# An attention and highway kernel on one core: fp32 dummy matmuls, wider key-value products for batch 0, weights cast in blocks of 128 rows, and a new list of steps

## The chip, the cores and the metric

The kernel runs on one core of one Trainium2 chip. The time is what the device takes for one execution, in microseconds (us); smaller is better. The core has five engines with queues of their own: TensorE (PE in the profile, its weight loads PEld), VectorE (DVE), ScalarE (ACT), GpSimd (POOL) and SyncE (SP), which here only issues transfers. 16 DMA engines carry the transfers.

## What is computed

```python
# q, k, v: (8 batches, 8 heads, 576 rows, 64), fp32
q_s = softmax(q, axis=-1)
k_s = softmax(k, axis=2)                     # over the 576 rows
kv  = einsum('bhsd,bhse->bhde', k_s, v)
x   = einsum('bhsd,bhde->bhse', q_s, kv)     # then (8*576, 512): a row is all heads of one token
H   = maximum(x @ w_h, 0)
T   = 1 / (1 + exp(-(x @ w_t + b_t)))
out = T * H + (1 - T) * x                    # (4608, 512), fp32
```

## The kernel before

**Tiles.** The 4,608 tokens are cut into 36 tiles of 128. Each pair of batches makes nine tiles: four of the first batch, four of the second, and one that shares the last 64 rows of both. Products are in fp16 with fp32 sums. Batch 0 and 1 are taken in halves (pairs of heads), so that work can begin before all of a batch has landed.

**Steps.** Everything is a list of named steps, ORDER (line 16). A loop at the end of the kernel walks through it and emits each step's instructions (`does`, from line 512). The scheduler is off: on each engine the instructions stand in the order of the list, and an engine takes them strictly one after another, so the list sets the order of all queues, that of SP included. A step is written `kind_batch_part` or `kind_tile_part`; a letter behind a colon chooses the engine (A is ScalarE, D VectorE, P GpSimd; F means all of it in one instruction).

Per batch *b*:
- `k`, `v`, `q` (lines 181 to 206): SP issues the loads. Batch 0 and 1 come in pieces, named by the first of their head pairs (`v_0_3`) or of their column groups (`q_0_4`). `w_h`, `w_t` (L208) load a weight in two halves of 256 rows, 512 KB each.
- `ek` (L253): ACT takes the exponential of k. `vc` (L259): a cast of v to fp16, beside a column of ones.
- `kv` (L262 to 272): PE multiplies, in products of 64x65 over rows: two row halves times two heads, four quarters of the array. A half of batch 0 or 1 is 36 such products. `kr` and `kn` (L281, L287) divide by the sums.
- `eq` (L307, 302, 298), `qt`, `qc` (L319 and 324, L333): the exponential of q, its turning on PE, the copy out of PSUM.

Per tile *i*:
- `xu` (L361) multiplies by kv; `rs`, `x` (L370, L376) divide, on DVE. `xt` (L384) turns x on PE, `xe` (L391) copies it to SBUF as xT.
- `bw` (L399, L401) puts the bias into the gate's PSUM; `mt` (L411) and `mh` (L419) are the two big products, four matmuls of 512 columns each. `th` takes a tanh on ACT (L433, L435), `dd` (L439) the maximum on DVE, `uu` the gate product, on DVE (L453) or, "lifted", as two instructions on POOL (L450, L451), `oo` (L471) the sum, on POOL, `st` the store, issued by SP.

**Weights.** `whd` (L226) subtracts the identity from a diagonal block of w_h, `whc` (L232) casts it to fp16 with a factor 0.5, `wtc` (L222) casts w_t. A cast takes 256 rows as 128x1024.

**Fills.** `fill_n` (L167) issues n matmuls of a blank tile into an otherwise unused PSUM buffer. They compute nothing that is kept. PE runs 40 of them up to 16.8 us.

**Buffers.** Tiles rotate in pools: three xT, three each of d16, rs, u16 and others in `dp`, six x16, one PSUM buffer shared by `kv` and `xu`.

Of the kernel before, what the change touches and what calls it, by code (L numbers as in the profile page):

```python
# [533 lines left out]
```

## Time and profile before

| | |
|---|---|
| median of 3 runs | 118.77 us (118.72 to 118.85) |
| the profiled execution's own time | 118.69 us |
| its span, first to last instruction | 116.9 us |
| granted PE clock, mean | 0.995 |
| busy: PE, DVE, ACT, POOL | 109.5, 93.3, 90.0, 89.1 us |
| DMA | 40.58 MB, mean 347 GB/s |
| start of kv_1_1, kv_2, kv_3, kv_4, kv_5, kv_6, kv_7 on PE | 23.24, 38.84, 48.7, 59.0, 66.2, 76.2, 92.8 us |
| start of PE's last matmul; end of the last `oo` | 111.8; 113.47 us |

The span is what the trace covers; 1.8 us of the profiled execution's time lie around it. Rows of 40 digits cut the span into slices of 2.9 us, each digit the busy share in tenths. A PE matmul's duration includes its way through the array and overlaps with the next one's, so its cost in a stream is the distance to the next start: 0.216 us for 512 columns, against a duration of 0.379. A landing is the moment at which a load's semaphore has its full count.

### The profile page before, as it was taken

To read this page: it belongs to the slowest core of one execution; us is meant where nothing else is said; L and a number is where in the kernel's file an instruction comes from. 1 tells how busy PE (TensorE), PEld (TensorE's weight loads), DVE (VectorE), ACT (ScalarE), POOL (GpSimd) and SP (SyncE) were. 2 spreads that over 40 slices of the span, in tenths; PEclk is the share of its full clock that TensorE was granted. 3 is DMA by queue.
4 is the path that set the end of the run, shared out by engine and by line. 5 is a ranking of instruction groups with operands and counts; after the bars stand their busy time and mean duration, and the time that the engine had idled before them with its cause. 6 is when DMAs were issued, how large, how long until landed. Compare 5 with 4: busy or idle time off the path is not lost.

```text
span 116.9 us, 3424 instructions
## 1 busy us (share of the span) xinstructions
PE 109.5 (94%) x1351; PEld 61.6 (53%) x1351; DVE 93.3 (80%) x222; ACT 90.0 (77%) x132; POOL 89.1 (76%) x99
## 2 busy tenths in 40 slices
PE   5999987999999999999999999999999999999930
PEld 2354544545665656565665547566564555554520
DVE  5642587589799979979889798988989887899870
ACT  4356461897999999989999999998597998545520
POOL 5022237208996999999999999999989699999960
PEclk9999999999999999999999999999999999999998
DMA  2999999999999999999999999999999956992875
GB/s 42 399 392 377 408 398 385 375 377 379 393 391 397 383 391 393 358 375 387 357 376 360 387 392 363 390 381 383 399 398 217 302 204 270 397 404 115 315 295 179
DMA packets 24195, 40.58 MB, mean 347 GB/s; under 512 B 5362, under 2 KB 11762, under 8 KB 24180
## 3 DMA queue, kind: packets, MB, share of 16 engines
q1 hardware_dynamic: 24032, 40.24, 96.9%
q8 instruction: 10, 0.16, 0.6%
q10 hardware_dynamic: 148, 0.14, 0.4%
q14 instruction: 5, 0.04, 0.1%
HBM read 30.41 MB, written 9.44 MB: 341 GB/s over the span
## 4 chain that ended last, share of the span: by engine, by line
PE 67%; POOL 15%; issue 6%; DVE 5%; DMA 3%; SPq 1%; POOLq 0%; DVEq 0%
PE tps L411 18%; PE gps L419 16%; PE turned L167 9%; POOL o L471 7%; PE xu L361 6%; PE turned L384 5%; PE kv L269 5%; PE qps L324 4%; POOL u L451 4%; DMA out_dram<-o 3%; POOL g L450 2%; PE qps L319 2%; POOL v L259 2%; DVE x L376 2%; PE tps L401 1%
## 5 line engine op out<-in xcount | busy, mean ns | idle before, releaser
L471 POOL TENSOR_TENSOR o<-u,x 128x512 f32<-128x512 f16 (+1 forms) x36 | 40.6, 1143 | 1.6 <-DVE u L453 0.7
L411 PE MATMUL tps<-w16t,xT 128*128 128x512 f16 (+1 forms) x148 | 37.3, 373 | 0.0
L419 PE MATMUL gps<-w16h,xT 128*128 128x512 f16 x144 | 36.8, 379 | 0.5 <-DVE xT L391 0.5
L376 DVE TENSOR_TENSOR x<-xu,rs 128x512 f16<-128x512 f32 (+1 forms) x39 | 25.2, 649 | 2.4
L259 POOL CAST v<-v 128x1152 f16<-128x1152 f32 (+1 forms) x14 | 14.0, 1010 | 14.7 <-DMA v<-in_v_dram 13.7
L439 DVE SCALAR_TENSOR_TENSOR d<-x,gps 128x512 f16<-128x512 f16 x36 | 24.5, 680 | 0.3
L451 POOL TENSOR_TENSOR u<-g,d 128x512 f16<-128x512 f16 x17 | 19.7, 1158 | 1.7 <-DVE rs L370 0.4
L253 ACT ACTIVATE ek<-k 128x576 f16<-128x576 f32 (+2 forms) x15 | 17.9, 1225 | 3.0 <-DMA k<-in_k_dram 3.0
L419 PEld LDWEIGHTS <-xT 128*128 128x128 f16 x144 | 13.0, 98 | 12.3 <-DVE xT L391 1.8
L399 ACT COPY tps<-ball 128x512 f32<-128x512 f32 x28 | 16.6, 597 | 3.5 <-DVE u L453 3.2
L411 PEld LDWEIGHTS <-xT 128*128 128x128 f16 x148 | 13.2, 98 | 10.6 <-DVE xT L391 0.4
L361 PE MATMUL xu<-kvb,eq 128*128 128x130 f16 (+1 forms) x160 | 14.8, 224 | 0.2 <-DVE kvb L287 0.2
L384 PE MATMUL turned<-idh,x 128*128 128x128 f16 x144 | 14.2, 220 | 0.5 <-DVE x L376 0.5
L391 DVE COPY xT<-turned 128x512 f16<-128x512 f16 (+1 forms) x28 | 10.9, 391 | 4.2 <-PE turned L384 3.0
L435 ACT ACTIVATE tps<-tps 128x512 f32<-128x512 f32 (+1 forms) x20 | 11.2, 559 | 3.6 <-PE tps L411 3.3
L453 DVE SCALAR_TENSOR_TENSOR u<-tps,d 128x512 f16<-128x512 f32 (+1 forms) x19 | 12.7, 671 | 1.4 <-ACT tps L435 0.6
L361 PEld LDWEIGHTS <-eq 128*128 128x128 f16 (+1 forms) x160 | 10.0, 100 | 7.3 <-DVE x L376 2.5
L167 PE MATMUL turned<-blank 128*128 128x512 f16 x40 | 12.4, 458 | 1.5 <-POOL blank L149 1.3
L384 PEld LDWEIGHTS <-x 128*128 128x128 f16 x144 | 9.8, 98 | 6.0 <-DVE x L376 2.1
L307 ACT ACTIVATE qe<-q 128x1024 f16<-128x1024 f32 (+3 forms) x9 | 9.4, 1052 | 4.1 <-DMA q<-in_q_dram 4.1
L450 POOL TENSOR_SCALAR g<-th 128x512 f16<-128x512 f16 x17 | 10.6, 621 | 0.9 <-ACT th L433 0.9
L433 ACT ACTIVATE th<-tps 128x512 f16<-128x512 f32 x17 | 10.0, 594 | 0.9 <-PE tps L411 0.9
(48 smaller groups left out, 106.8 us busy)
## 6 DMA issues: line engine op xcount, KB each, us to landing
k<-in_k_dram SPq DMA_DIRECT2D x6, 1152.0 KB, 12.2
v<-in_v_dram SPq DMA_DIRECT2D x6, 1152.0 KB, 12.0
out_dram<-o SPq DMA_DIRECT2D x23, 256.0 KB, 4.0
q<-in_q_dram SPq DMA_DIRECT2D x10, 512.0 KB, 11.5
out_dram<-o SPq DMA_DIRECT2D x6, 512.0 KB, 3.8
k<-in_k_dram SPq DMA_DIRECT2D x4, 576.0 KB, 9.3
q<-in_q_dram SPq DMA_DIRECT2D x2, 1152.0 KB, 14.2
q<-in_q_dram SPq DMA_DIRECT2D x2, 640.0 KB, 10.5
```

The costliest lines, as they stand in the source:

```text
L167: nc.tensor.matmul(spare, blank[:, 0:P], blank, start=True, stop=True, skip_group_check=True)
L253: nc.scalar.activation(t[:, :, c:c + n].rearrange("p j c d -> p c j d"), T[f"k32{b}"][:, c:c + n].rearrange("p c (j d) -> p c j d", j=NJ), ...
L259: copy(v16[b % NV][:, c:c + n, :, 0:D], T[f"v32{b}"][:, c:c + n].rearrange("p c (j d) -> p c j d", j=NJ))
L361: nc.tensor.matmul(dst, turned_q(b, jp, n), kvb[b % NKV][:, hh, kk], start=True, stop=True, skip_group_check=True)
L376: nc.vector.tensor_mul(t[:, k0:k1], sums(i, k)[:, :, :, 0:64], T[f"rs{i}_{k}"][:, 0:k1 - k0].unsqueeze(3).to_broadcast([P, k1 - k0, 4, D]))
L384: nc.tensor.matmul(t[:, n], T[f"x{i}"][:, n0 + n % 2:n0 + 2 * P:2], idh, is_transpose=True, start=True, stop=True, skip_group_check=True)
L399: nc.scalar.copy(t[:, cs], ball[:, cs])
L411: nc.tensor.matmul(T[gate(i, k)][:, cs], T[f"xT{i}"][:, n], w16["t"][:, n, cs], start=False, stop=(n == parts[-1] and not first), skip_gro ...
L419: nc.tensor.matmul(t, T[f"xT{i}"][:, n], w16["h"][:, n], start=(first and n == parts[0]), stop=(n == parts[-1] and not (first and len(part ...
L439: nc.vector.scalar_tensor_tensor(t, T[f"x{i}"], -0.5, T[f"gps{i}"], op0=ALU.mult, op1=ALU.max)
L451: nc.gpsimd.tensor_mul(t, g, T[f"d{i}"])
L471: eng.tensor_add(t[:, cs], T[f"u{i}_{h}"][:, cs], T[f"x{i}"][:, cs])
```

## The change

- **Fills.** `blank` is fp32 now. `fill_n` issues one matmul for every four units, of 128 columns a unit. An fp32 matmul has no weight load of its own in the list. The list has 36 units in 11 instructions, before 40 in 80 (matmul and weight load).
- **Batch 0's products.** One product takes two heads at once: 64 rows, 128 output rows, 130 columns. Half of what it computes (each head's keys with the other head's values) is not read. A half batch is 18 products and 18 weight loads, before 36 and 36. `kr` and `kn` follow the new layout.
- **Weights.** A cast step takes one block of 128 rows: 128x512 instead of 128x1024. Its engines are chosen anew: w_t three times POOL and once ACT, w_h three times ACT and once DVE; two of four `whd` on DVE, before all four on POOL.
- **Buffers.** Five xT instead of three, five d16 instead of three.
- **The list** is new throughout. w_t is loaded ahead of w_h; batch 0's second half is loaded and multiplied first; PE's first weight products are mt_1 and mt_3, before mh_1 and mh_3; q_1_0 is loaded ahead of v_1_2. Up to v_3 the list loads the same set; then v_4 follows k_4 and v_7 follows k_7. 19 tiles are lifted to POOL (before 17); vc_6_0 and vc_7_0 are on ACT (before POOL). PE's program has 2,561 rows (before 2,704).

```diff
@@ -14,50 +14,50 @@
 ORDER = """
-b_0 q_0_0 v_0_1 setupdve k_0_0 b_32 eq_0_0 bsplit setuppool fill_5 fill_8 bp v_0_0 bc qt_0_0 ek_0_1 v_0_3 ek_0_0 k_0_2
-v_0_2 vc_0_3:A bw_1 vc_0_0 ek_0_2 vc_0_2 q_0_4 vc_0_1:D ek_0_3 bw_0 w_h_0 fill_8 qc_0_0 whd_1:P kv_0_0 eq_0_1 w_h_2
-w_t_2 kr_0_0 whd_0:P whd_2:P w_t_0 k_1_2 v_1_2 q_1_0 k_1_0 v_1_0 fill_5 q_1_4 kn_0_0 q_2_0 k_2_0 eq_0_2 xu_0_0 v_2_0
-q_3_0 rs_0_0 whc_0:A x_0_0 k_3_0 fill_4 v_3_0 kv_0_1 fill_3 kr_0_1 kn_0_1 xu_0_1 rs_0_1 xu_1_0 rs_1_0 qt_0_1 x_1_0
-fill_6 whd_3:P qc_0_1 xt_1_0 xu_3_0 qt_0_2 qc_0_2:A xe_1_0:D fill_1 rs_3_0 x_3_0 x_0_1 xt_3_0 xu_2_0 rs_2_0 x_2_0
-wtc_2:P whc_2:A mh_1_0 wtc_0:P vc_1_3 ek_1_3 ek_1_2 vc_1_0 xe_3_0:D mh_3_0 dd_1 xt_0_1 xt_0_0 mt_1_0 xe_0_0:D mh_0_0
-xe_0_1 dd_3 xt_2_0 mh_0_1 mt_0_1 th_1_0 xe_2_0:D dd_0 vc_1_2:A kv_1_1 uu_1_0 oo_1_0 eq_1_0 mt_0_0 th_0_0 ek_1_0 ek_1_1
-kr_1_1 bw_3 qt_1_0 vc_1_1:A kn_1_1 qc_1_0 mt_3_0 xu_5_1 uu_0_0 mh_2_0 th_3_0 bw_2 rs_5_1 x_5_1 dd_2 xu_4_1 kv_1_0
-kr_1_0 eq_1_1 rs_4_1 xt_5_1 mt_2_0 th_2_0 kn_1_0 bw_5 xe_5_1:D x_4_1 xu_5_0 mt_5_1 qt_1_1 eq_1_2 rs_5_0 x_5_0 xt_5_0
-xu_4_0 bw_4:A uu_3_0:P oo_3_0 xe_5_0:D mh_5_1 rs_4_0 x_4_0 mh_5_0 xt_4_1 qc_1_1:A xt_4_0 xe_4_1:D dd_5 eq_2_0 xe_4_0:D
-v_4_0 mt_5_0 th_5_0 xu_6_0 qt_1_2 rs_6_0 qc_1_2 oo_0_0 mt_4_1 mh_4_1 mh_4_0 uu_2_0:P x_6_0 mt_4_0 eq_2_1 xt_6_0 xu_8_0
-uu_5_0 bw_6:A xe_6_0:D qt_2_0 rs_8_0 x_8_0 mh_6_0 oo_5_0 th_4_0 xt_8_0 dd_4 uu_4_0 xu_7_0 mt_6_0 ek_2_0:F rs_7_0
-vc_2_2:A bw_8 xe_8_0:D mt_8_0 x_7_0 th_6_0 xt_7_0 th_8_0 oo_2_0 vc_2_0 kv_2_0 oo_4_0 qc_2_0 q_4_0 bw_7:A qt_2_1
-qc_2_1:A dd_6 uu_6_0:P oo_6_0 eq_3_0:F xe_7_0:D kr_2_0 kn_2_0 mh_8_0 xu_9_0 rs_9_0 x_9_0 mt_7_0 th_7_0 bw_9 dd_8
-uu_8_0:P qt_2_2 qc_2_2:A xu_10_0 bw_10:A xt_9_0 xe_9_0:D rs_10_0 x_10_0 ek_3_0 mh_7_0 dd_7 ek_3_2 mh_9_0 xu_12_0 k_4_0
...
-dd_30 mh_33_0 oo_31_0 bw_33:A rs_34_0 xt_32_0 x_34_0 th_30_0 xe_32_0:D qc_7_2:A uu_30_0 mt_33_0 st_28_0 st_31_0
-mh_32_0 dd_33 th_33_0 uu_33_0 xu_35_0 bw_32:A rs_35_0 oo_33_0 xt_34_0 mt_32_0 bw_34:A xe_34_0:D mh_34_0 st_33_0 x_35_0
-xt_35_0 mt_34_0 dd_32 th_32_0 bw_35_1 oo_30_0 st_16_0 st_30_0 uu_32_0 xe_35_0 oo_32_0 mh_35_0 th_34_0 bw_35_0 mt_35_0
-th_35_0 mt_35_1 dd_34 uu_34_0 oo_34_0 dd_35 uu_35_0 st_32_0 th_35_1 uu_35_1 st_34_0 oo_35_0 st_35_0 oo_35_1:D
+b_0 b_32 setupdve setuppool fill_3 fill_8 bsplit bp q_0_0 eq_0_0 qt_0_0 k_0_2 v_0_2 vc_0_2:D v_0_3 fill_8 vc_0_3 k_0_0
+v_0_1 bc bw_1 v_0_0 vc_0_0 q_0_4 w_t_0 wtc_0:P qc_0_0 w_t_2 wtc_2:P ek_0_2 wtc_3:P ek_0_3 w_h_0 kv_0_1 kr_0_1 kn_0_1
+fill_6 vc_0_1:D bw_3 ek_0_0 xu_0_1 ek_0_1 kv_0_0 kr_0_0 kn_0_0 eq_0_1 fill_6 xu_0_0 rs_0_0 x_0_0 w_h_2 k_1_2 xu_1_0
+eq_0_2 qt_0_1 whd_2:P fill_5 rs_1_0 x_1_0 q_1_0 qc_0_1:A xt_1_0 qt_0_2 xu_3_0 whd_1:P rs_0_1 xe_1_0:D wtc_1 mt_1_0
+rs_3_0 x_3_0 xt_3_0 v_1_2 th_1_0 k_1_0 whd_0 whc_0:A xe_3_0:D qc_0_2 bw_0 mt_3_0 whd_3 x_0_1 whc_2:A whc_1:D whc_3:A
+xt_0_0 v_1_0 ek_1_3 vc_1_2 xt_0_1 q_1_4 th_3_0 xe_0_0 xu_2_0 mh_1_0 rs_2_0 xe_0_1:D mt_0_1 dd_1 x_2_0 eq_1_0 mh_3_0
+dd_3 uu_3_0 ek_1_2 vc_1_3:D mh_0_0 mh_0_1 dd_0 xt_2_0 xe_2_0 qt_1_0 mt_0_0 q_2_0 bw_2 qc_1_0:A th_0_0 uu_1_0:P vc_1_0
+ek_1_1 kv_1_1 kr_1_1 kn_1_1 ek_1_0 oo_3_0 mt_2_0 uu_0_0:P oo_1_0 xu_5_1 rs_5_1 vc_1_1:A x_5_1 k_2_0 xt_5_1 xe_5_1:D
+xu_4_1 rs_4_1 x_4_1 kv_1_0 kr_1_0 kn_1_0 bw_5 th_2_0 mt_5_1 xu_5_0 rs_5_0 v_2_0 xu_4_0 bw_6 eq_1_1 qt_1_1 x_5_0 rs_4_0
+eq_1_2 xt_5_0 xe_5_0:D mh_2_0 mt_5_0 q_3_0 k_3_0 x_4_0 xt_4_0 dd_2 xt_4_1 qc_1_1:A xu_6_0 mh_5_1 mh_5_0 xe_4_0 rs_6_0
+xe_4_1:D qt_1_2 th_5_0 bw_4 oo_0_0 eq_2_0:F v_3_0 qc_1_2 uu_2_0:P q_4_9 mh_4_1 mt_4_1 x_6_0 q_4_0 ek_2_0 dd_5 uu_5_0:P
+xu_8_0 xt_6_0 mt_4_0 th_4_0 rs_8_0 oo_5_0 x_8_0 qt_2_0 mh_4_0 xe_6_0:D xu_7_0 mh_6_0 mt_6_0 qc_2_0 dd_4 xt_8_0 rs_7_0
+x_7_0 uu_4_0 ek_2_2 xe_8_0:D qt_2_1 qc_2_1 vc_2_2:A vc_2_0 kv_2_0 kr_2_0 kn_2_0 dd_6 oo_2_0 th_6_0 bw_8:A k_4_0 xt_7_0
+xe_7_0:D qt_2_2 mt_8_0 xu_9_0 rs_9_0 x_9_0 mh_8_0 dd_8 mh_7_0 xt_9_0 bw_9:A qc_2_2:A xe_9_0:D v_4_0 oo_4_0 uu_6_0:P
+oo_6_0 eq_3_0 xu_10_0 eq_3_1 th_8_0 qt_3_0 rs_10_0 x_10_0 qc_3_0 mh_9_0 xu_12_0 k_5_0 rs_12_0 uu_8_0:P xt_10_0 bw_7:A
...
+bw_30:A xu_34_0 oo_31_0 xt_32_0 xe_32_0:D th_33_0 bw_32:A mh_33_0 st_28_0 mt_30_0 rs_34_0 x_34_0 th_30_0 st_31_0
+xu_35_0 dd_30 xt_34_0 xe_34_0 mt_32_0 mh_32_0 dd_33 uu_30_0 rs_35_0 x_35_0 mh_34_0 th_32_0 dd_32 uu_32_0 uu_33_0:P
+oo_33_0 oo_30_0 st_33_0 st_30_0 oo_32_0 xt_35_0 xe_35_0:D bw_34:A mt_34_0 th_34_0 bw_35_0 mt_35_0 mh_35_0 dd_34
+uu_34_0 dd_35 st_32_0 oo_34_0 st_34_0 th_35_0 uu_35_0 bw_35_1 mt_35_1 th_35_1 uu_35_1 oo_35_0 st_35_0 oo_35_1:D
 st_35_1:A
 """
@@ -90,7 +90,7 @@
     qep = pool("qep", 2)
     eqp = pool("eqp", 4)
     xp = pool("xp", 6)
-    xtp = pool("xtp", 3)
+    xtp = pool("xtp", 5)
     dp = pool("dp", 3)
     op = pool("op", 7)
     PS = bass.MemoryType.PSUM
@@ -108,7 +108,7 @@
     b16 = consts.tile([P, DM], FP16, name="b16")
     ball = consts.tile([P, DM], FP32, name="ball")
     ones = consts.tile([P, P], FP16, name="ones")
-    blank = consts.tile([P, DM], FP16, name="blank")
+    blank = consts.tile([P, DM], FP32, name="blank")
     NKV, NV = 3, 2
     kvb = [consts.tile([P, 2, 2, 130], FP16, name=f"kvb{i}") for i in range(NKV)]
     v16 = [consts.tile([P, 4, NJ, 66], FP16, name=f"v16_{i}") for i in range(NV)]
@@ -163,9 +163,11 @@
             nc.vector.memset(v16[i][:, :, :, 64:66], 1.0)
 
     def fill(e, n):
-        for _ in range(n):
-            nc.tensor.matmul(spare, blank[:, 0:P], blank, start=True, stop=True,
+        while n:
+            m = min(n, 4)
+            nc.tensor.matmul(spare[:, 0:P * m], blank[:, 0:P], blank[:, 0:P * m], start=True, stop=True,
                              skip_group_check=True)
+            n -= m
 
 
     source = dict(k=k, q=q, v=v)
@@ -215,21 +217,16 @@
 
 
     def wt_cast(e, c):
-        if e == "D":
-            nc.vector.tensor_scalar_mul(w16["t"][:, c:c + 2], T[f"wt{c}"], 1.0)
-        else:
-            copy = nc.gpsimd.tensor_copy if e == "P" else nc.scalar.copy
-            copy(w16["t"][:, c:c + 2], T[f"wt{c}"])
+        copy = dict(D=nc.vector.tensor_copy, P=nc.gpsimd.tensor_copy).get(e, nc.scalar.copy)
+        copy(w16["t"][:, c], T[f"wt{c // 2 * 2}"][:, c % 2])
 
     def wh_less_identity(e, c):
         block = T[f"wh{c // 2 * 2}"][:, c % 2, c // 2 * 2 * P + c % 2:c // 2 * 2 * P + 2 * P:2]
         (nc.gpsimd if e == "P" else nc.vector).tensor_sub(block, block, idf)
 
     def wh_cast(e, c):
-        if e == "D":
-            nc.vector.tensor_scalar_mul(w16["h"][:, c:c + 2], T[f"wh{c}"], 0.5)
-        else:
-            nc.scalar.mul(w16["h"][:, c:c + 2], T[f"wh{c}"], 0.5)
+        mul = nc.vector.tensor_scalar_mul if e == "D" else nc.scalar.mul
+        mul(w16["h"][:, c], T[f"wh{c // 2 * 2}"][:, c % 2], 0.5)
 
     def bsplit(e):
         for r in (0, 32):
@@ -259,11 +256,20 @@
         copy(v16[b % NV][:, c:c + n, :, 0:D], T[f"v32{b}"][:, c:c + n].rearrange("p c (j d) -> p c j d", j=NJ))
 
 
+    BROAD = (0,)
+
     def kv(e, b, k):
         ps = once(f"kvps{b}", lambda: ps_x.tile([P, 2, DM], FP32, tag="xu", name=f"kv_{b}"))
         for kk in range(*halves(b, k)):
             for j in range(NJ):
                 for hh in range(2):
+                    if b in BROAD:
+                        rows, heads_ = slice(64 * hh, 64 * hh + 64), slice(2 * kk, 2 * kk + 2)
+                        nc.tensor.matmul(
+                            ps[:, hh, 130 * kk:130 * kk + 130],
+                            T[f"ek{b}"][rows, j, heads_].rearrange("p c d -> p (c d)"), v16[b % NV][rows, heads_, j, 0:65],
+                            start=(j == 0), stop=(j == NJ - 1), skip_group_check=True)
+                        continue
                     for w in range(2):
                         rows, cols = slice(64 * hh, 64 * hh + 64), slice(64 * w, 64 * w + 64)
                         nc.tensor.matmul(
@@ -273,20 +279,22 @@
 
     def kv_of(b, k):
         k0, k1 = halves(b, k)
-        return T[f"kvps{b}"][:, :, 0:130].rearrange("p h (k e) -> p h k e", k=2)[:, :, k0:k1]
+        n = 2 if b in BROAD else 1
+        return T[f"kvps{b}"][:, :, 0:130 * n].rearrange("p h (k w e) -> p h k w e", k=2, w=n)[:, :, k0:k1]
 
     def kr(e, b, k):
         k0, k1 = halves(b, k)
-        rz = T[f"rz{b}_{k}"] = dp.tile([P, 2, 2], FP32, tag="rz", name=f"rz_{b}_{k}")
-        nc.vector.reciprocal(rz[:, :, 0:k1 - k0], kv_of(b, k)[:, :, :, 64])
+        n = 2 if b in BROAD else 1
+        rz = T[f"rz{b}_{k}"] = dp.tile([P, 2, k1 - k0, n], FP32, tag="rz", name=f"rz_{b}_{k}")
+        nc.vector.reciprocal(rz, kv_of(b, k)[:, :, :, :, 64])
 
     def kn(e, b, k):
         k0, k1 = halves(b, k)
         for w in range(2):
-            r, e0 = slice(64 * w, 64 * w + 64), 65 * w
+            r, e0, n = slice(64 * w, 64 * w + 64), 65 * w, w if b in BROAD else 0
             nc.vector.tensor_mul(
-                kvb[b % NKV][r, :, k0:k1, e0:e0 + 64], kv_of(b, k)[r, :, :, 0:64],
-                T[f"rz{b}_{k}"][r, :, 0:k1 - k0].unsqueeze(3).to_broadcast([64, 2, k1 - k0, 64]))
+                kvb[b % NKV][r, :, k0:k1, e0:e0 + 64], kv_of(b, k)[r, :, :, n, 0:64],
+                T[f"rz{b}_{k}"][r, :, :, n].unsqueeze(3).to_broadcast([64, 2, k1 - k0, 64]))
 
 
     GROUPS = ((0, 4), (4, 8), (8, 9))
@@ -435,7 +443,7 @@
             nc.scalar.activation(src, src, AF.Tanh, scale=0.5)
 
     def dd(e, i):
-        t = T[f"d{i}"] = dp.tile([P, DM], FP16, tag="d16", name=f"d16_{i}")
+        t = T[f"d{i}"] = dp.tile([P, DM], FP16, tag="d16", bufs=5, name=f"d16_{i}")
         nc.vector.scalar_tensor_tensor(t, T[f"x{i}"], -0.5, T[f"gps{i}"], op0=ALU.mult, op1=ALU.max)
 
     def uu(e, i, h):
```

## The prediction

> **What bounds the kernel now.** I read the page's busy shares first, then the chain of work that ended last, then TensorE's (PE's) waits after 20 us, then the DMA queues beside the landing times.
>
> ```profile
> PE 109.5 (94%) x1351; PEld 61.6 (53%) x1351; DVE 93.3 (80%) x222; ACT 90.0 (77%) x132; POOL 89.1 (76%) x99
> ...
> PE   5999987999999999999999999999999999999930
> ...
> DMA  2999999999999999999999999999999956992875
> ...
> q1 hardware_dynamic: 24032, 40.24, 96.9%
> q8 instruction: 10, 0.16, 0.6%
> ```
>
> Two things are full at once: PE from slice 8 to the end, and the DMA engines up to slice 30. A busy PE row can hide waiting, so I read the chain for start-to-start distances. Here is the stretch ahead of batch 2's key-value product:
>
> ```profile
> 35.34 0.86 PE gps L419 x4
> 36.20 0.22 PE turned L384 x4
> 36.42 0.23 PE xu L361 x4
> 36.66 0.86 PE tps L411 x4
> 37.52 0.22 PE tps L401
> 37.74 0.94 PE tps L411 x4
> 38.68 0.22 PE turned L384 x4
> 38.90 0.73 PE kv L269 x63
> 39.63 0.55 PE qps L324 x8
> ```
>
> Four matmuls of 512 columns always take 0.86 us (0.216 each), four turns 0.22: PE streams without a hole. PE's waits after 20 us hold one row of 0.5 us. Adding start-to-start times from kv_2 (38.84) to the last matmul (111.8), 72.5 us are work and about 0.6 us are holes. So whatever pins kv_2, plus PE's work behind it, sets the end. What pins it:
>
> ```profile
> 37.54 1.15 ACT L259 CAST v<-v 128x1152 f16<-128x1152 f32 x1
> ...
> 37.64 1.15 POOL L259 CAST v<-v 128x1152 f16<-128x1152 f32 x1 [0.95 <-PE tps L411]
> ...
> 38.84 0.35 PE L269 MATMUL kv<-v,ek 64*64 64x65 f16 x20
> ```
>
> v_2 landed at 37.52, both casts of it start at once, end at 38.69 and 38.79, and PE starts kv_2 0.05 us later. Landings follow each other by 3.0 us per 1,152 KB from 28 us on, so they cannot come sooner by being issued sooner (v_2 was issued at 23.04).
>
> One hole in the landings matters. The trace has ten packets of 16,384 bytes on q8 (instruction), of 1.0 to 1.2 us each, the first at 15.17 us, when 275 PE instructions had started; the next at 27.12 (486), 37.98 (735), 45.99 (1008): about one in 256 instructions. Each load's landing is counted in 16 parts. For w_h_2 all 16 lie within 14.60 to 15.06. For w_t_2, the next, 15 lie within 15.89 to 16.34 and one at 17.64. That part stays about 1.3 us behind in nearly every load after it, so loads landed 1.3 us late from 16 us on. Later packets put other parts behind, and the largest lag then grows little (v_2: twelve parts by 35.78, the last 37.52).
>
> **The change, part by part.** I add to the profiled execution's own 118.69 us (span 116.9, and 1.8 around it); the median of the runs is 0.08 above it.
>
> 1. *Fewer PE instructions.* 40 fills of two instructions become 11 of one, batch 0's 144 products 36. In the new list the 256th PE instruction is the last of mt_0_0, just ahead of kv_1_1, near 24 us; in the old one it stands in qt_0_1 (14.2 to 14.6). So the lag of 1.3 us should leave w_h_0, w_h_2, k_1, q_1_0, v_1 and return from about 24 us. q_1_4 (before: 15 parts by 26.95, last 28.24) and v_2 come after that and still land late. Not seen: whether the first packet then lags as much. Bounds for v_2: at best 35.85 plus the first lag alone (about 1.4): 37.25, at worst 37.52. I take 37.37, the middle: -0.15.
>
> The Trainium skill ("Runtime: NRT & Kernel Launch", Instruction fetch mechanics) states that instructions come in blocks of 16 KiB, 256 of them, and that the cost of crossing a block is mostly hidden. The packets agree (16,384 bytes); the landings do not (17.64 against 16.34). By that rule this term is nothing, and the sum would be 0.15 us higher.
>
> 2. *fp32 fills.* 36 units instead of 40, in instructions of up to 512 columns standing for four units each. No row shows an fp32 matmul. The rows near it: one 128x512 fp16 takes 0.216 warm (0.427 up to 6.7 us), its weight load 0.098. Low end: one instruction as one fp16 pass, 36 units in 9 x 0.216 = 1.9 us, and PE idles instead. High end: four passes with four exposed loads, 4 x (0.216 + 0.098) = 1.26, in all 11.3 us, against 40 x 0.216 = 8.6 now: +2.7. I take four passes behind hidden loads, 0.86, the row it replaces: -0.9 early.
>
> The Trainium skill ("FP8 and Floating Point Precision", TensorE Precision Notes) gives true fp32 four passes through the array. By that the fill is the 0.86 that I took.
>
> The fp32 blank is twice the bytes. A memset of 128x128 took 0.205 in f32 and 0.205 in f16, so 0.53 as now; at worst +0.5, covered since PE's first real work waits for b16 (5.73) and qe (5.74).
>
> 3. *Batch 0's products.* 36 of 64x65 took 0.41. Now 18 of 130 columns per half: between 0.52 (the two row halves side by side, as different quarters start 0.003 apart now) and 1.03 (18 x 0.057, the xu row). I take 0.52, since it is the kv row that shares the array: +0.1 a half, at worst +0.6.
>
> 4. *Weights in blocks of 128 rows.* w_t lands first now. A POOL cast of 1,024 columns took 1.04; 576 took 0.67, so 512 about 0.6. w16t is whole at about 16.3 (w_t_2 at 15.06, two casts), and mt_1 starts there; before, PE's first weight product was mh_1 at 18.14. mh_1 now waits for w_h_2: 17.6, two subtractions of 0.46 on POOL, casts to about 19.7. Two subtractions and a cast go to DVE (0.3 to 0.5 each), which was busy 6.6 of 9 us there: covered. whd_0 and whd_3 add waits for w_h there: behind them queue xe_3, qc_0_2 and x_0_1, and PE's mt_3 waits for xe_3; if they hold DVE, mt_3 comes later by as much, inside the lead below.
>
> 5. *What the lead is worth.* At mh_1, in list order, PE is some 1.5 us ahead of the old schedule. Then two things stop it. qt_1_1 needs q_1_4: 28.24, plus eq_1_1 of 1.06, so 29.45; before it ran at 29.80, with 0.6 us less of PE's work behind it. So of the lead 0.35 is kept there and 0.6 is owed. Then kv_2: v_2 at 37.37, cast 1.15, so 38.6 to 38.7 against 38.84. All of 2, 3 and 4 ends in that cover of about 1 us.
>
> 6. *PE's work behind kv_2.* Newly behind it: mt_8 (0.86) and xt_7 (0.22). No longer: bw_9 (0.22, now ACT's) and qt_2_1 (0.45). +0.42, with nothing beside it: PE has no holes to take it in.
>
> 7. *The rest of the list.* Summed by rows, POOL has two v casts fewer (-2.3), smaller w casts and two subtractions fewer (-1.2), and two lifted tiles more (+2 x 1.78): +0.1. ACT gains two 1.15 casts and loses two of 0.66 and smaller ones; DVE gains about 1 us of its 23 idle. On SP, v_4 moves behind k_4 and v_7 behind k_7; counted by bytes v_4 lands near 56 and v_7 near 88.5, 2 us or more ahead of their kv steps. xT and d16 get two buffers more, which can only take waits away; I find none on PE to take: 0, between -0.6 (all the holes) and +0.6 (as many new).
>
> 8. *Tail.* mh_35 now stands behind mt_35's first half, not ahead of it. DVE then runs dd_35 (0.68), two uu (0.42 each) and oo (0.42) after mh_35 ends, about 0.27 us before the last matmul does; before, dd_35 was done at 112.13 and waited for th. By DVE's distances the last oo ends 1.8 us after the last matmul's start, against 1.65 now: +0.15.
>
> Sum: 118.69 - 0.15 + 0.42 + 0.15 = **119.1 us**.
>
> **Rivals.**
>
> *Faster (27%).* v_2's sixteenth part lands with the others, because the packet at 24 us meets a DMA engine with slack, or it is fetched at another time. For it: for loads up to 15 us all parts come within 0.46 us. Against: the second packet of before did put parts behind. Price: 37.52 to 35.85 is -1.67, so 118.69 - 1.67 + 0.57 = 117.6 at most, if qt_1_1 does not hold; with half of it 118.4. It turns the sign from 0.57 us of earlier landing.
>
> *Holes closed (10%).* The deeper xT and d16 pools and the new list take the 0.6 us out: 118.5.
>
> *fp32 fills too long, or the clock (8%).* At the high end +2.7 early less a cover of 1: 120.8. The same place breaks if idle PE keeps the 0.427 spacing past 6.7 us.
>
> *The fetch does not move (7%).* If an fp32 matmul is fetched as several instructions, w_h and k_1 stay late and term 1 is nothing: 119.3.
>
> **How the numbers follow.** Forecast 48%, its own range 118.75 to 119.6. A measurement of this kernel can tell some 0.2% (0.24 us) from no change, so 118.53 to 119.01 is the same: of the forecast 13 of 48 points lie there, 35 above. Faster rival: 25 faster, 2 same. Holes closed: 5 and 5. Fills: 8 slower. Fetch: 2 same, 5 slower. Together faster 0.30, same 0.22, slower 0.48. The range 117.8 to 120.0 leaves out half of the faster rival's far end and most of the long fills.
>
> **What would show it.** The first q8 packet near 24 us and w_h_2's parts together near 17.6: term 1. The fill's spacing: 2. mt_1 near 16.4, mh_1 near 19.7: 4. eq_1_1 and the two casts of v_2 starting right at landings, and PE waiting ahead of qt_1_1 or kv_2: 5. The last matmul 73 us or a little more after kv_2: 6 and 7. dd_35 after mh_35: 8. I am wrong if kv_2 starts before 38.3, or if the time from kv_2 to the last matmul is under 72.7 or over 74 us.

## The result

The changed kernel takes 119.53 us (median of 4 runs, 119.38 to 119.74) where the kernel before takes 118.79 beside it: a ratio of 1.0063, 95% interval 1.0046 to 1.0081. Taken again on another chip, in 11 runs, it came out at 1.0058 (1.0038 to 1.0079). So the change costs 0.7 us. The forecast was 119.1, slower; the profiled executions, which the sum was made for, took 119.38 after and 118.69 before: +0.69, where the sum had +0.42.

### The profile page after: what moved, and what is told of

Its sections match the earlier page's. It is cut to its first block, busy times and chain, and to the rows that moved or that the text cites. A ratio compares the mean times of both kernels' runs of the same rounds, so it can differ in the third digit from the quotient of the medians.

```text
span 117.6 us, 3321 instructions
## 1 busy us (share of the span) xinstructions
PE 108.2 (92%) x1297; PEld 62.4 (53%) x1297; DVE 94.6 (80%) x226; ACT 90.7 (77%) x132; POOL 89.1 (76%) x100
## 4 chain that ended last, share of the span: by engine, by line
PE 75%; DMA 13%; DVE 4%; ACT 2%; issue 1%; SPq 1%; DVEq 0%; ACTq 0%
PE gps L427 26%; PE tps L419 24%; DMA w32h<-in_moe_w_h_dram 8%; PE turned L392 7%; PE xu L369 7%; DMA v<-in_v_dram 5%; PE kv L275 4%; PE qps L332 3%; PE qps L327 2%; ACT w16h L229 1%; SPq L185 1%; DVE x L384 1%; PE tps L409 1%; DVE d L447 1%; ACT ek L250 1%
## 5 line engine op out<-in xcount | busy, mean ns | idle before, releaser
L427 PE MATMUL gps<-w16h,xT 128*128 128x512 f16 x144 | 36.0, 379 | 0.0
L459 POOL TENSOR_TENSOR u<-g,d 128x512 f16<-128x512 f16 x19 | 22.0, 1155 | 2.0 <-DVE d L447 0.6
L256 POOL CAST v<-v 128x1152 f16<-128x1152 f32 (+1 forms) x12 | 11.7, 984 | 13.6 <-DMA v<-in_v_dram 8.6
L441 ACT ACTIVATE th<-tps 128x512 f16<-128x512 f32 x19 | 11.4, 598 | 2.9 <-PE tps L419 2.8
L458 POOL TENSOR_SCALAR g<-th 128x512 f16<-128x512 f16 x19 | 11.7, 618 | 1.9 <-ACT th L441 1.9
L443 ACT ACTIVATE tps<-tps 128x512 f32<-128x512 f32 (+1 forms) x18 | 10.0, 558 | 4.0 <-PE tps L419 4.0
L461 DVE SCALAR_TENSOR_TENSOR u<-tps,d 128x512 f16<-128x512 f32 (+1 forms) x17 | 11.4, 672 | 1.1 <-ACT tps L443 0.2
L168 PE MATMUL turned<-blank 128*128 128x512 f32 (+3 forms) x22 | 10.5, 611 | 1.3 <-POOL blank L149 1.3
```

Of the source, the lines that this page charges most:

```text
L256: copy(v16[b % NV][:, c:c + n, :, 0:D], T[f"v32{b}"][:, c:c + n].rearrange("p c (j d) -> p c j d", j=NJ))
L427: nc.tensor.matmul(t, T[f"xT{i}"][:, n], w16["h"][:, n], start=(first and n == parts[0]), stop=(n == parts[-1] and not (first and len(part ...
L458: nc.gpsimd.tensor_scalar(g, T[f"th{i}"], 1.0, 1.0, op0=ALU.add, op1=ALU.mult)
L459: nc.gpsimd.tensor_mul(t, g, T[f"d{i}"])
```

## The profile after

The page of the changed kernel, the same rows as were shown of before:

```profile
PE 108.2 (92%) x1297; PEld 62.4 (53%) x1297; DVE 94.6 (80%) x226; ACT 90.7 (77%) x132; POOL 89.1 (76%) x100
...
PE   5998998796999999999999999999999999999930
...
DMA  2999999999999999999999999999999980999275
...
q1 hardware_dynamic: 24032, 40.24, 95.9%
q8 instruction: 10, 0.16, 0.6%
```

PE's row has new dents at slices 8 and 10 (of 2.94 us each: 20.6 to 23.5 and 26.5 to 29.4 us); from slice 11 on it is full, as before. The DMA row is full up to slice 32, as before. Next the chain ahead of batch 2's key-value product (start, length, what):

```profile
36.70 0.86 PE gps L427 x4
37.57 0.86 PE tps L419 x4
38.43 0.22 PE turned L392 x4
38.65 0.45 PE qps L332 x8
39.10 0.71 PE kv L275 x66
```

PE still streams without a hole, but what it waited for there has changed. In the timeline:

```profile
37.61 1.15 ACT L256 CAST v<-v 128x1152 f16<-128x1152 f32 x1
...
37.65 1.14 POOL L256 CAST v<-v 128x1152 f16<-128x1152 f32 x1 [0.19 <-DMA v<-in_v_dram]
...
39.03 0.78 PE L275 MATMUL kv<-v,ek 64*64 64x65 f16 x72
```

v_2 landed at 37.52, as before, and its casts ended at 38.76 and 38.79 (before: 38.69 and 38.79). But kv_2 starts at 39.03, 0.24 after the later cast: PE itself came late. The list of PE's waits after 18 us (us in all, times, longest) tells where. First the one row of before (its 0.5 us end at 19.67, ahead of the 20 us from which the prediction counts it), then the rows of after:

```profile
PE gps L419 <- DVE xT L391: 0.5, 1, 0.5
```

```profile
PE turned L392 <- DVE x L384: 0.7, 1, 0.7
PE tps L419 <- DVE xT L399: 0.7, 1, 0.7
PE tps L409 <- ACT th L441: 0.5, 1, 0.5
PE xu L369 <- DVE kvb L295: 0.4, 1, 0.4
```

And by stretches, PE's busy time from 20 to 31 us, first in the kernel before, then after (us, then PE, PEld, DVE, ACT, POOL busy, clock, DMA share, GB/s):

```profile
20.00:31.00 11.00, 11.00 (x144) 5.69 (x142) 8.42 (x25) 9.28 (x16) 4.99 (x7) 1.00 1.06 380
```

```profile
20.00:31.00 11.00, 9.15 (x131) 4.86 (x130) 7.95 (x24) 8.67 (x15) 6.69 (x8) 1.00 1.06 385
```

**Work left.** To compare two lists, I price every PE record at its warm cost (0.216 us for 512 columns, in proportion; a batch's key-value products 0.82; fills nothing) and add up what has not started yet at a given time. Both kernels have 94.39 us of it in all. us of useful PE work left:

| at (us) | 20 | 27 | 31 | 34 | 39 | 48 | 80 | 110 |
|---|---|---|---|---|---|---|---|---|
| before | 89.13 | 82.56 | 79.01 | 76.10 | 71.32 | 62.40 | 31.27 | 1.84 |
| after | 87.83 | 82.56 | 79.66 | 76.74 | 71.98 | 63.05 | 31.86 | 2.59 |
| after, minus before | -1.30 | 0 | +0.65 | +0.64 | +0.66 | +0.65 | +0.59 | +0.75 |

The new kernel is 1.30 us ahead at 20 us, level at 27 and 0.65 behind at 31. From 31 us on the difference stays within 0.1 us: nearly all of it is made between 20 and 31 us, where 1.95 us of lead go.

## The experiments

All ratios are to the kernel before on the same chip, by medians; kv_2, the way from it to the last matmul and the tail (end of the last `oo` less the last matmul's start) are from one profiled execution each. In before they are 38.84, 72.98 and 1.66 us, after 39.03, 73.49 and 1.81.

| kernel | ratio (95%) | kv_2 | to last matmul | tail |
|---|---|---|---|---|
| after, again | 1.0058 (1.0038 to 1.0079) | 38.96 | 73.47 | 1.81 |
| new code, old list | 1.0020 (1.0004 to 1.0037) | 39.23 | 73.22 | 1.66 |
| old code, new list | 1.0163 (1.0140 to 1.0185) | 40.63 | 74.02 | 1.80 |
| old tail | 1.0032 (1.0017 to 1.0047) | 39.46 | 73.34 | 1.64 |
| many short fills | 1.0118 (1.0096 to 1.0139) | 40.54 | 73.34 | 1.81 |
| old list to kv_2, then new | 1.0205 (1.0174 to 1.0237) | 39.84 | 74.98 | 1.81 |
| new list to kv_2, then old | 1.0140 (1.0110 to 1.0170) | 39.06 | 74.79 | 1.67 |
| holes filled | 1.0154 (1.0121 to 1.0186) | 41.94 | 73.40 | 1.64 |
| more ahead of kv_2 | 1.0119 (1.0091 to 1.0147) | 40.71 | 73.22 | 1.67 |
| and xe_3, mh_5_1 earlier | 1.0114 (1.0088 to 1.0140) | 40.08 | 73.24 | 1.66 |
| v_1 before q_1 | 1.0291 (1.0252 to 1.0330) | 42.48 | 73.37 | 1.81 |
| holes filled, bank freed | 1.0064 (1.0039 to 1.0089) | 39.59 | 73.49 | 1.64 |

### The code and the list apart

New code, old list: fills, products, casts of 128 rows and pools as after, the steps in the order of before.

```diff
-(the list of after)
+(the list of before, with the casts of 128 rows where that of 256 stood:)
+... whc_0:A whc_1:A x_0_0 ... wtc_2:P wtc_3:P whc_2:A whc_3:A mh_1_0 wtc_0:P wtc_1:P ...
```

> The kernel after with the list of steps of the kernel before; fp32 fills, two heads at once for batch 0, casts of 128 rows and the wider pools stay. Theory L (the list costs the time: 0.19 up to kv_2, 0.51 from kv_2 to the last matmul, 0.15 in the tail, and whatever the code does early is covered by the landing of v_2): 118.6 to 118.9, like the kernel before, with kv_2 at 38.7 to 38.9 and the last oo 1.66 after the last matmul's start. Rival C (the new code costs the time: the fills, the longer halves of batch 0, the casts): 119.3 to 119.6. Rival B (the code gains and the list loses more): below 118.4, with kv_2 before 38.5.

Old code, new list:

```diff
-    xtp = pool("xtp", 5)
+    xtp = pool("xtp", 3)
-    blank = consts.tile([P, DM], FP32, name="blank")
+    blank = consts.tile([P, DM], FP16, name="blank")
-            nc.tensor.matmul(spare[:, 0:P * m], blank[:, 0:P], blank[:, 0:P * m], start=True, stop=True,
+            nc.tensor.matmul(spare, blank[:, 0:P], blank, start=True, stop=True,
-    BROAD = (0,)
+    BROAD = ()
-        t = T[f"d{i}"] = dp.tile([P, DM], FP16, tag="d16", bufs=5, name=f"d16_{i}")
+        t = T[f"d{i}"] = dp.tile([P, DM], FP16, tag="d16", name=f"d16_{i}")
```

> The kernel before in its fills (fp16, one instruction a unit), its products of batch 0 (one head at a time) and its pools, with the new list of steps and the casts of 128 rows that the list names. Theory L: 119.4 to 119.9, as slow as the kernel after or a little slower, since the last 74 us are those of the kernel after and only the first 39 us can differ. Rival C: 118.6 to 118.9, like the kernel before. Rival B: 119.9 or more.

The new code alone costs 0.0020 of 119, so 0.2 us. The new list alone costs 1.9 us. Together they cost 0.7. So the parts do not add up: the code (fills, products and pools; the casts of 128 rows are in both runs) is worth some 1.2 us to the new list and nothing to the old one. Theory L had the list as the price, which holds in the main (it had nothing for the code, which costs 0.2), but also that nothing early counts, which fails by 1.2 us; rival C falls; B has the signs nearest, though the code gains nothing by itself. In the old list PE still waits for v_2 ahead of kv_2, as step 5 of the prediction described it for the new one; the chain of waits in that run:

```profile
23.20 14.72 DMA v<-in_v_dram
...
38.04 1.15 POOL v L256
...
39.23 0.80 PE kv L275 x67
```

kv_2 starts right behind the cast of v_2, which landed at 37.92 in this execution; PE had 0.34 us beyond its price there, where a key-value product with nothing to wait for has 0.1. By the work left there is no lead to lose in this run: 89.35 us at 20 us against 89.13 in before, 79.23 at 31 against 79.01. Its kv_2 is later than in before because v_2 landed 0.40 later; its loads ran late from the first on (q_0_0 by 0.4).

### What the fills' few instructions are worth

The same fill work at the same price on PE, as 288 PE instructions (matmul and weight load) instead of 11:

```diff
-        while n:
-            m = min(n, 4)
-            nc.tensor.matmul(spare[:, 0:P * m], blank[:, 0:P], blank[:, 0:P * m], start=True, stop=True,
+        for _ in range(4 * n):
+            nc.tensor.matmul(spare[:, 0:P], blank[:, 0:P], blank[:, 0:P], start=True, stop=True,
```

> The kernel after with each unit of its fills as four fp16 products of 128 columns, 288 in all instead of 11 fp32 ones, so that TensorE's first packets of instructions are fetched at about 4 and 13 us instead of 19.21. If a packet makes one part of a landing late: w_h_0, w_h_2, k_1 and q_1_0 have one part 1.3 to 1.5 us behind, as in the kernel before. Theory L (v_2's landing covers the early part): the times at mt_1 and mh_1 go up by up to 1.4 us, kv_2 by no more than 0.4, the whole by 0 to 0.4 (119.5 to 119.9). Rival: a lead or a delay of the first 20 us counts in full: about 120.8.

The first packets came at 12.31 and 19.56 us, not at 4 and 13. The landings did what was expected: w_t's second half has 15 parts by 15.02 and the last at 16.73, w_h's halves the last at 18.01 and 19.30, where after has all parts by 16.38 and 17.66. mh_1 starts at 20.60 instead of 19.62, and PE's waits have one longer row:

```profile
PE tps L417 <- DVE xT L397: 1.2, 1, 1.2
```

Of that delay nothing is taken in on the way: kv_2 is 1.5 us later than after, the last matmul 1.4 later. By medians the kernel is 0.7 us slower than after (1.0118 against 1.0058 and 1.0063). Theory L fails here too, and its rival is right: in the new list an early delay is paid in full. This is also most of the 1.2 us that the new code is worth to the new list. The old code with the new list, whose first packet also comes early (15.44), differs from this kernel in the products of batch 0, the pools and fills of 512 columns; it is 0.5 us slower by medians, all of it behind kv_2 (74.02 against 73.34, with holes of 0.32 and 0.28 us at 68.7 and 84.4 that the other runs of the new list lack). The pools were not tried alone, so that they are its cause is an argument, not shown.

The prediction weighed a sentence of the Trainium skill ("Runtime: NRT & Kernel Launch", Instruction fetch mechanics) by which the cost of crossing a block of instructions is mostly hidden. On PE's own queue it is hidden here too: PE streams on through the packet at 12.31 us. In the loads it is not: with the first packet at 12.3 instead of 19.2 us the time is 0.7 us longer.

### The tail

```diff
-xt_35_0 xe_35_0:D bw_34:A mt_34_0 th_34_0 bw_35_0 mt_35_0 mh_35_0 dd_34
+xt_35_0 xe_35_0:D bw_34:A mt_34_0 th_34_0 bw_35_0 mh_35_0 mt_35_0 dd_34
```

> The kernel after with mh_35 ahead of mt_35's first half, as in the kernel before; nothing else moves. If the tail's 0.15 us is the place of mh_35: 0.15 less than the kernel after (119.35 to 119.42), and the last oo ends about 1.66 after the last matmul's start instead of 1.81. If the 0.15 has another cause (the slower arrival of dd_35's inputs whatever their order): no change, 1.8 again.

The timeline's end, after (the last `dd`, the last products, the last `oo`):

```profile
112.19 0.60 PE L419 MATMUL tps<-w16t,xT 128*128 128x256 f16 x4
112.29 0.69 DVE L447 SCALAR_TENSOR_TENSOR d<-x,gps 128x512 f16<-128x512 f16 x1
...
113.91 0.42 DVE L479 TENSOR_TENSOR o<-tps,x 128x256 f32<-128x256 f32 x1
```

and with the old tail:

```profile
112.41 0.68 DVE L447 SCALAR_TENSOR_TENSOR d<-x,gps 128x512 f16<-128x512 f16 x1
112.47 0.60 PE L419 MATMUL tps<-w16t,xT 128*128 128x256 f16 x4
...
114.01 0.42 DVE L479 TENSOR_TENSOR o<-tps,x 128x256 f32<-128x256 f32 x1
```

dd_35 starts ahead of the last four matmuls instead of behind the first of them, and the last `oo` ends 1.64 instead of 1.81 after the last matmul's start: the tail's term is 0.17. By medians the kernel is 0.3 us faster than after (1.0032 against 1.0058), with intervals that overlap; the trace has the size. The new code with the old list ran on the same chip, 12 runs each: 119.25 us there, 119.42 here, again with intervals that overlap. So with the old tail the new list is within 0.2 us of the old one under the same code, and of the 0.7 us the code by itself is about 0.2, the tail 0.15 to 0.3, the rest of the list about 0.2.

### Where in the list

After once more, to have its scatter and its ratio on a second chip:

> The kernel after once more, unedited, so that the kernels beside it are compared on one chip: 1.006 of the kernel before. If the profiled span moves by 0.2 to 0.5 us against its first profile, the moment at which TensorE's clock doubles should move with it (4.9 us in the first), and kv_2 by the same amount.

The ratio is that of the first chip, and so is the profile (kv_2 at 38.96, tail 1.81), which was taken in the fastest of its 11 runs (119.27, of up to 120.14). Its span moved by 0.1 us only, so it does not test what was expected of the clock; the other kernels' profiles say more, at the end.

Two lists spliced at kv_2, with the code of after: the steps of one list up to kv_2, then all that is left in the order of the other.

```diff
-(all of the list after)
+(the list of before up to kv_2_0, then what is left in the order of the list after)
```

> The code of the kernel after; the list of before up to kv_2, then the steps that are left in the order of the list after. Theory P (the list costs by what stands ahead of and around kv_2; the order of the last 74 us costs nothing): kv_2 to the last matmul as in the run of the new code with the old list (73.0 to 73.2), and 0.15 more in the tail: 1.002 to 1.004 of before. Rival Q (the order of the last 74 us is itself slower): 73.5 or more and 1.006.

```diff
-(all of the list after)
+(the list after up to kv_2_0, then what is left in the order of the list of before)
```

> The code of the kernel after; its list up to kv_2, then the steps that are left in the order of the list before. Theory P: kv_2 where the kernel after has it, 73.3 to 73.5 from there to the last matmul since the work moved behind kv_2 stays behind it, 0.15 less in the tail: 1.004 to 1.006 of before. Rival Q: 73.0 and about 1.002.

Neither theory is right: both spliced lists are slower than both whole ones, and take 74.8 to 75.0 us from kv_2 to the last matmul. The useful work left shows why: between 39 and 48 us they lose 0.9 (new, then old) and 2.0 us more than after does, in holes of 0.94, 0.87 and 0.80 us at 41.9 to 42.9, where what one list had put behind kv_2 stands beside what the other had already done. A list is one piece; splices say little about its parts, and I drew nothing else from these two.

### Filling the holes

The two holes at 27.4 and 29.4 us are these pieces of the chain of waits, after:

```profile
26.41 0.23 PE xu L369 x2
...
26.88 0.43 DVE x L384
...
27.36 0.30 PE turned L392 x2
...
28.70 0.28 DVE kvb L295
...
29.00 0.31 DVE kvb L295
...
29.35 0.41 PE xu L369 x4
```

PE has run out of work that does not depend on batch 1 and follows DVE: divide x_5_1, turn it; normalize kv_1, multiply by it. But mh_2, whose operand is there since 24.5, stands in the list behind qt_1_1, at 30.5. So I moved it.

```diff
-xu_5_1 rs_5_1 vc_1_1:A x_5_1 k_2_0 xt_5_1 xe_5_1:D xu_4_1 rs_4_1 x_4_1 kv_1_0 kr_1_0 kn_1_0 ...
+xu_5_1 mh_2_0 rs_5_1 vc_1_1:A x_5_1 k_2_0 xt_5_1 xe_5_1:D xu_4_1 rs_4_1 kv_1_0 kr_1_0 kn_1_0 x_4_1 ...
-... vc_2_0 kv_2_0 ... xt_7_0
+... vc_2_0 xt_7_0 kv_2_0 ...
```
(with the old tail)

> The kernel after with TensorE's holes at 27.4 and 29.4 us filled (mh_2 behind xu_5_1; kv_1, kr_1 and kn_1 ahead of x_4_1), xt_7 ahead of kv_2, and the tail of before. Theory P: kv_2 waits for v_2's casts again (38.8 to 39.0), the work behind it is 0.2 less, the tail 0.15 less: 0.4 to 0.6 less than the kernel after, 1.001 to 1.003 of before. Rival (the holes were covered, kv_2 stays): only the tail's 0.15 and up to 0.2, about 1.004 of before.

It went the other way. PE's waits:

```profile
PE xu L369 <- DVE x L384: 1.3, 2, 0.7
```

In the halved tiles `xu` takes its PSUM from the same two banks as `mh` (`ps_g`, two buffers). mh_2 held one of them (a bank, one buffer of this memory) from 26.5 until dd_2 read it at 32.2, so xu_5_0 and xu_4_0 had to share the other, each waiting for the x before it. And then the clock fell:

```profile
31.00:36.00 5.00, 4.61 (x30) 2.62 (x29) 1.98 (x8) 3.69 (x4) 3.64 (x5) 0.66 1.05 386
```

The clock column reads 0.66 where after has 1.00, and 512 columns take 0.427 us again at 33.5 to 34.4. kv_2 came at 41.94. The profiled execution is one of two among seven with a mean granted clock of 0.986 (122.1 and 122.3 us); the other five, at 0.993 to 1.000, took 120.7 to 121.2. So I estimate some 1.3 us of the profiled time for the fallen clock, and the median, which is one of the five, is still 1.0 us above after on the same chip (120.81 against 119.86).

Mended: dd_2 right behind xt_5_1, so that the bank is free for xu_5_0, and the steps around qt_1_1 arranged to match.

```diff
-xu_5_1 rs_5_1 vc_1_1:A x_5_1 k_2_0 xt_5_1 xe_5_1:D xu_4_1 rs_4_1 x_4_1 kv_1_0 kr_1_0 kn_1_0 bw_5 th_2_0 mt_5_1 xu_5_0 rs_5_0
-v_2_0 xu_4_0 bw_6 eq_1_1 qt_1_1 x_5_0 rs_4_0 eq_1_2 xt_5_0 xe_5_0:D mh_2_0 mt_5_0 ... dd_2 xt_4_1 qc_1_1:A xu_6_0 mh_5_1 mh_5_0
+xu_5_1 mh_2_0 rs_5_1 vc_1_1:A x_5_1 k_2_0 xt_5_1 dd_2 xe_5_1:D xu_4_1 kv_1_0 kr_1_0 kn_1_0 rs_4_1 x_4_1 bw_5 th_2_0 mt_5_1 xu_5_0 rs_5_0
+v_2_0 bw_6 eq_1_1 qt_1_1 xu_4_0 x_5_0 xt_4_1 xt_5_0 xe_5_0:D rs_4_0 eq_1_2 mh_5_1 mt_5_0 ... qc_1_1:A xu_6_0 mh_5_0
```
(with xt_7 ahead of kv_2 and the old tail as above)

> The kernel with the filled holes, mended: mh_2 behind xu_5_1 as there, but dd_2, which frees mh_2's bank, right behind xt_5_1, kr_1 and kn_1 ahead of rs_4 and x_4's second half, xu_4's first half behind qt_1_1, and xt_4_1 and mh_5_1 between qt_1_1 and mt_5_0; xt_7 ahead of kv_2 and the old tail as there. Theory H (TensorE's holes between 20 and 31 us are the loss): the holes at 27.4 and 29.4 shrink by 0.9 or more in sum, the useful work left at 31 us falls from 78.7 to 77.8 to 78.2, kv_2 waits for v_2's casts at 38.7 to 38.9, and the time is 0.3 to 0.6 less than the kernel after: 1.001 to 1.004 of before. If filled holes come back as waits at another place ahead of kv_2: kv_2 at 39.0 or later and 1.005 or more, of which the tail accounts for 0.15 less.

The two holes close to 0.26 us at 29.5, PE's busy time from 20 to 31 us rises from 9.15 to 10.17, and the work left at 31 us falls to 79.12 by the table's prices. But the time does not follow: 1.0064. The second branch of what I had written is what happened. The kernel with the old tail is the one to compare with, since its profiled execution began equally late (mt_1 at 16.80 and 16.73):

| useful PE work left at | 31 | 34 | 39 | 48 |
|---|---|---|---|---|
| old tail | 80.09 | 77.18 | 72.31 | 63.48 |
| holes filled, bank freed | 79.12 | 76.74 | 71.98 | 63.80 |

0.97 us are won by 31 us. By 34 a half is gone. The largest piece is a hole of 0.35 us at 33.2 (0.18 of it idle), at another pair of banks, that of the gates: the bias of tile 4 waits until tile 5's tanh has read its gate, because tile 6's bias, put ahead of qt_1_1, holds the other.

```profile
PE tps L409 <- ACT th L441: 0.6, 2, 0.5
```

(of the two times the longer is at 18 us, as after). 0.33 is still there at 39, and then xt_7, which I had moved ahead of kv_2, loses it and as much again: PE waits 0.36 us at 39.3 for the turned tile ahead of it to be copied, and the next `xu` 0.42 at 41.7 for kv_2's normalization. So the holes are real, but filled in this way they are worth a third of their size, and my own move spent that. Without that move I estimate 0.5 less (0.36 and 0.42, less the 0.06 that this `xu` waits anyway and the 0.22 of xt_7 behind kv_2 again), some 1.002 of before; it was not run.

### Two more ways to use the lead

In the old list, PE's wait ahead of kv_2 filled:

```diff
-... vc_2_0 kv_2_0 ... kn_2_0 mh_8_0 xu_9_0 rs_9_0 x_9_0 mt_7_0
+... vc_2_0 mh_8_0 kv_2_0 ... kn_2_0 mt_7_0 xu_9_0 rs_9_0 x_9_0
```

> The new code with the old list (which came out at 1.002 of before, with TensorE waiting 0.34 us for v_2's casts ahead of kv_2), and mh_8 put ahead of kv_2, mt_7 ahead of xu_9. If that wait is where the early gain of the new code goes: the wait is filled, 0.2 to 0.35 less than that run: 0.999 to 1.000 of before. Rival (xu_9 then waits for kn_2, which mh_8 covered): 1.002 or more.

The same, and 0.66 us saved at 19.9:

```diff
-xu_2_0 rs_2_0 x_2_0 ... xe_3_0:D mh_3_0 ... xu_5_0 mt_5_1 qt_1_1 ... xe_5_0:D mh_5_1
+xu_2_0 xe_3_0:D rs_2_0 x_2_0 ... mh_3_0 ... xu_5_0 mt_5_1 mh_5_1 qt_1_1 ... xe_5_0:D
```

> As the kernel with mh_8 ahead of kv_2, and xe_3 ahead of rs_2 on VectorE (TensorE waited 0.66 us for it at 19.9) and mh_5's second half ahead of qt_1_1. If TensorE's work left at 31 us decides the time: the 0.4 to 0.5 saved at 19.9 us is still there at 31 us, and the time is 0.3 to 0.5 less than with mh_8 alone: 0.995 to 0.998 of before. Rival (another wait between 20 and 31 us, the landing of q_1's second part above all, takes it): the same as with mh_8 alone.

Both came out at 1.011 to 1.012: the rivals, and worse. The wait was filled, and a new one of 0.93 us opened at 44.3 (43.6), where an `xu` waits for the x that frees the one buffer of `ps_x` (mh_8 ahead of kv_2, its row of the waits):

```profile
PE xu L369 <- DVE x L384: 0.8, 1, 0.8
```

More telling is the second kernel's work left: 88.59 at 20 us (new code with the old list: 89.35), 0.7 less, of which 0.2 was there ahead of the change (mh_1 at 18.19 against 18.41); 85.26 at 24 (85.48); 79.23 at 31 (79.23). In the old list whatever is won before 20 us is gone by 24 to 31 us, with a new wait of 0.65 at 22.1.

And v_1 ahead of q_1 in the new list, to have kv_1's first half sooner:

```diff
-... x_1_0 q_1_0 ... xt_3_0 v_1_2 ... x_2_0 eq_1_0 mh_3_0 ... vc_1_3:D mh_0_0 mh_0_1 dd_0 xt_2_0 xe_2_0 qt_1_0 mt_0_0 ... kv_1_1 kr_1_1 kn_1_1 ...
+... x_1_0 v_1_2 ... xt_3_0 q_1_0 ... x_2_0 mh_3_0 ... vc_1_3:A mh_0_0 mh_0_1 dd_0 kv_1_1 kr_1_1 kn_1_1 xt_2_0 xe_2_0 eq_1_0 mt_0_0 ... mt_2_0 qt_1_0 qc_1_0:A ...
```

> The kernel after with v_1's first load back ahead of q_1's, its last cast on ScalarE, kv_1's first half (with kr_1, kn_1) ahead of xt_2, and eq_1 and qt_1 later to match. If TensorE's holes of 0.90 and 0.59 us at 27.4 and 29.4 come from kv_1's first half being 1.7 us later than in the kernel before (24.91 against 23.24, behind a landing 1.5 us later): the holes shrink by 0.6 to 1.5 in sum, the useful work left at 31 us falls from 78.7 to 77.7 to 78.2, and the time is 0.3 to 0.7 less than the kernel after: 1.000 to 1.004 of before. Rival (the holes have another source): no change, 1.006.

kv_1's first half came 1.0 us sooner (23.93), but eq_1 and qt_1, put off to make room, came too late: xu_5_1 waits at 28.9 for ScalarE's copy of qt_1, a hole of 2.1 us; kv_1's second half came at 30.27 instead of 27.69, and the clock fell to 0.51 between 31 and 34 us (five of the six executions have a mean of 0.978 to 0.980). So this run does not answer its question: the order of the loads was changed along with the work on ScalarE that hangs on it. Whether the swapped loads make the holes stays open.

## Why the prediction was right, and where it was not

1. *Fewer PE instructions (-0.15).* The size failed, to 0: v_2 landed at 37.52 again. The packet came at 19.21 us, not near 24. An fp32 matmul stands in the trace as two matmul and two weight-load records, so the 11 fills are 44 and the 256th record starts at 22.63 instead of 24.17. That is a third of the error. The rest is the count itself: first packets came after 273 records before, 221 after, 200 with the new code and old list, 300 with many short fills, so one in 256 was too exact for this step. The rival of 7% (the fetch does not move) had its condition right, a fill being several instructions, and its time, 119.3, nearest to the 119.38 of the profiled execution; but w_h and k_1, which it had late, were not. What the step said of w_h_0, w_h_2 and k_1 (all parts together by 16.38, 17.66 and 19.17) was right; q_1_0 has its lag again (21.99).
2. *fp32 fills.* The price was right: 0.853 a warm instruction, against the 0.86 taken. (The buffer they write is the one into which x is turned, `turned` in the rows, so it is not otherwise unused.)
3. *Batch 0's products.* 0.62 a half, inside the bounds and 0.1 above the value taken.
4. *Weights in blocks.* mt_1 at 16.36 and mh_1 at 19.62, as worked out (16.3 and 19.7).
5. *What the lead is worth.* This step failed. It let the lead of 1.5 us end in two stops set by landings, qt_1_1 and kv_2, with "all of 2, 3 and 4" under their cover: qt_1_1 at 29.45, 0.35 ahead of before, and kv_2 at 38.6 to 38.7. The landings did what it said: eq_1_1 ended at 29.44. But PE reached qt_1_1 only at 29.81 and kv_2 at 39.03, and waited for a landing at neither. (The 29.80 that the step gives for qt_1_1 in before is from the chain view, which counts from the end of the work ahead; by its start, as 29.81 is, it is 29.64. So qt_1_1 came 0.17 later than before, not 0.35 sooner.) On the way there PE waited for other engines: 0.85 us at 21.3, 0.90 at 27.4, 0.59 at 29.4. The last two are the round trips through DVE shown above; in the last, kv_1's normalization also stood behind x_4_1 on DVE until 28.6. The first comes from ACT, on which the three casts of w_h, an exponential of k and a tanh stand ahead of tile 0's first xT copy (the chain of waits from 15 to 22 us, after):

```profile
17.93 1.45 ACT w16h L229 x3
...
19.49 0.67 ACT ek L250
20.16 0.49 ACT tps L443
20.64 0.31 ACT xT L399
...
20.98 0.30 DVE xT L399
...
21.33 0.61 PE tps L419 x2
```

   PE came to kv_2 after v_2's casts, so no cover is left: the fills' instruction count, the clock's start and every hole count in the new list, as many short fills showed with 0.7 us by medians and 1.4 in the trace.
6. *Work behind kv_2 (+0.42).* 0.51 measured, 0.49 in the second profile. The count was right, but it was no cost of its own: the total of useful work is the same 94.39, and what stands behind kv_2 more stands ahead of it less. It is the work that PE could have done by 31 us and did not, seen from kv_2: the work left is 0.65 higher at 31 us and 0.66 at 39.
7. *The rest of the list (0).* Right: from 31 to 80 us the difference stays at 0.6 to 0.7.
8. *Tail (+0.15).* Right: 0.15, and 0.17 by the run that undid it.

By the terms: kv_2 +0.19 (forecast -0.15), to the last matmul +0.51 (+0.42), tail +0.15 (+0.15), in all +0.85 at the last `oo`; behind it 0.16 came back, since its end to the span's end took 3.27 instead of 3.43. The forecast was low by what it did not follow: it took landings and PE's sums through 20 to 31 us, and not ACT's queue, on which the first hole hangs, nor the round trips through DVE, on which the other two hang. That the time came out this near is in part luck: kv_2 was 0.34 us later than in the sum and the way from it to the last matmul 0.09 longer, and the 0.16 that came back at the end, which no term has, took part of that away.

What stays open: which of the list's choices between 20 and 34 us holds the level there; nothing was tried on the hole at 21.3 us, the first of the three, in the new list. Filling two holes won 0.97 us by 31 us and lost half of it by 34 to a PSUM bank; the order of loads was not separated from the rest. No kernel tried is faster than the kernel before.

## What to carry to other kernels

When an order is rewritten, compare the useful work left on the full engine at a few times, not one milestone: that shows at once in which stretch a lead is lost, and a term like "work behind kv_2" turns out to be the same loss told twice. Before counting on cover by a landing, check that the engine arrives before the landing, by following the queues of the other engines that it waits for on the way: if it arrives after, every early delay is paid in full. And a step moved forward also takes its PSUM bank forward: it must bring along the step that frees it.
